# Block-sparse attention with a squared-ReLU feed-forward: putting off more squares and moving one slot's choices from a transfer to the matmul engine

## The chip, the cores and the metric

The kernel runs on one core of a Trainium2 chip. The metric is the device time of one execution in microseconds (us), the median of several runs. Five engines work side by side, each through its own queue in order: PE (TensorE: matmuls, and transposes as matmuls against an identity), DVE (VectorE), ACT (ScalarE), POOL (GpSimd) and SP (SyncE, which here only issues transfers). POOL issues the loads that convert f32 to bf16; SP issues the transposing transfers and the stores.

## The reference

For 4 batches and 8 heads, 768 rows and head size 64, each query row keeps the 6 best of 24 chunks of 32 keys. The bound of a chunk is computed from the minimum and maximum of its keys. Attention runs over the kept chunks, causally, and a feed-forward with squared ReLU follows.

```python
k_chunks = k.reshape(B, H, nc, chunk, D)
k_min = np.min(k_chunks, axis=3)
k_max = np.max(k_chunks, axis=3)
ub = np.sum(np.maximum(q[:, :, :, None, :] * k_min[:, :, None, :, :], q[:, :, :, None, :] * k_max[:, :, None, :, :]), axis=-1)
ub = np.where(causal, ub, -1000000000.0)
top_chunks = np.argsort(ub, axis=-1)[..., -top_k:]
scores = scale * np.matmul(q, k.transpose(0, 1, 3, 2))
sel = (j_chunk == top_chunks[..., None]).any(axis=-2)
mask = sel & (pos[:, None] >= pos[None, :])
# softmax over the masked scores, then attn @ v; then, row by row of x (3072 x 512):
h = np.maximum(x @ w_in, 0.0)
return (h * h @ w_out).astype(np.float32)
```

## The kernel before

The work is cut into 8 half-batches `hb` (384 query rows of one batch) in a fixed `ORDER`, and each into 4 slots, one for each pair of heads: 32 slots `s`, with `hb = s // 4`. A slot has these steps, and the main loop writes out by hand in which order the steps of neighbouring slots follow one another in each engine's queue:

- `step_T` transposes k and q on PE (half-batches 0 to 2). From half-batch 3 on (`ON_PE = 3`) SP does it by transposing transfers (`tr`, L320), six for each half-batch: three tiles of k and three of q.
- `extrema` or `step_K` (DVE) make the chunks' minima and maxima; `relus_T` or `relus` (L316, L317) make the positive and negative parts of q.
- `step_U` computes the bounds `ub` on PE (L371 to L382). The DVE then takes the sixth largest (MAX8, L389) and compares (L391): a 1 for each chunk that is not chosen.
- These choices have to stand transposed under the transposed q in the operand `kq`, as 32 further rows of the contraction, where a large negative weight pushes the chunks that were not chosen out of the softmax. `step_V` does that on PE for half-batches 0 to 2: it transposes into PSUM (L424 or L434) and the DVE copies (L428 or L439). From half-batch 3 on `step_Q` (L405) puts the q beside the choices in `nsel`, and `step_W` (L413) sends both through a transposing transfer on SP.
- `step_E` computes the scores (L452, PE), the exponential (L458, ACT) and the causal diagonal (L462, POOL).
- `step_F` multiplies with v (L480, PE) and divides (L489, L490, DVE) into `x`. `x` is transposed by SP (L494), or in a few slots by PE in `x_T` (L518) with a DVE copy (L524).

The feed-forward of a finished half-batch is pushed into a `queue` of 16 "up" steps (`ffn_up`, one for each f: L566 on PE, the ReLU L576 on ACT, the square L577 on the DVE) and 12 "down" steps (`ffn_down`, L589). The calls `f1()` take one step of it at a time and so place it between the attention's steps; `quota` says how many a slot takes. For the last four f of half-batch 0 the ReLU goes straight into `h` (L572) and the square is put into a list `squares`, which is worked off (L573) in slot 8.

Loads are listed by slot in `later` and issued by `go(s, n)`, at most n of them at each call. SP's transposing transfers stand in `first` (issued at the start of a slot) and `by_sp`. PSUM tiles of `psA` (tag `att`) have two buffers, shared by `ub`, `po` and `qt`.

Of the kernel before, what the change touches and what calls it, by code (L numbers as in the profile page):

```python
# [9 lines left out]
BF16 = mybir.dt.bfloat16  # L10
# [6 lines left out]
HT = 3  # L17
HB = HT * 128
# [12 lines left out]
ON_PE = 3  # L31
# [8 lines left out]
def kernel(  # L40
# [9 lines left out]
    nc = tc.nc  # L50
    B, H, S, D = q.shape
    NC = S // CH
    NT = S // 128
    NP = H // 2
# [3 lines left out]
    NFI = DFF // 128  # L58
# [12 lines left out]
    CR = CH  # L71
# [172 lines left out]
    def step_cast(n, p):  # L244
        if n == "k":
            nc.vector.tensor_copy(packed("k", 0)[:, 2 * p:2 * p + 2], staged["k", p])
        else:
            nc.scalar.copy(qn0[:, :, p, :, 0:D], staged["q", p])
# [161 lines left out]
    def step_W(s):  # L410

        b, half, p = slots[s]
        nc.sync.dma_start_transpose(  # L413
            out=kqs[b % 2][:, p, 2 * half + 1].rearrange("r h (j t) -> r (h j) t", j=HT),
            in_=nsel[half][:, s % 2].rearrange("r h j n d -> r (h j n d)"))

    def step_V(s):
        b, half, p = slots[s]
        if s < NP:

            qt = psA.tile([128, 2, HB], BF16, tag="att", name="qt")
            for hh in range(2):
                for j in range(HT):
                    nc.tensor.matmul(  # L424
                        qt[0:KR, hh, 128 * j:128 * (j + 1)],
                        lhsT=qn0[:, j, p, hh, :],
                        rhs=ident, is_transpose=True, start=True, stop=True)
            nc.vector.tensor_copy(kqs[b % 2][0:KR, p, 2 * half + 1], qt[0:KR])  # L428
            return
        j0 = 1 - half  # L430
        c = 128 * j0
        qt = psA.tile([128, HB], BF16, tag="att", name="qt")
        for j in range(j0, HT):
            nc.tensor.matmul(  # L434
                qt[0:2 * CR, 128 * j:128 * (j + 1)],
                lhsT=chosen[s % 2][:, j].rearrange("r h c -> r (h c)"),
                rhs=ident, is_transpose=True, start=True, stop=True)
        for h in range(2):
            nc.vector.tensor_copy(  # L439
                kqs[b % 2][D:KR, p, 2 * half + 1, h, c:], qt[CR * h:CR * h + CR, c:])  # L440

    def step_E(s, hh, n):
        b, half, p = slots[s]
# [119 lines left out]
    def ffn_up(hb, xT, f):  # L563
        ph = psF.tile([128, 512], F32, tag="ph", name="ph")
        for ki in range(NKI):
            nc.tensor.matmul(  # L566
                ph[:, 0:HB], lhsT=w_in[:, ki, 128 * f:128 * (f + 1)],
                rhs=xT[:, ki, :], start=(ki == 0), stop=(ki == NKI - 1))
        h = late.tile([128, HB], BF16, tag="h", bufs=2 * NFI + 2, name="h")
        if hb == 0 and f >= NFI - 4:  # L570
            h2[hb, f] = h
            nc.scalar.activation(h, ph[:, 0:HB], ACT.Relu)  # L572
            squares.append(lambda: nc.vector.tensor_mul(h, h, h))  # L573
            return
        ht = late.tile([128, HB], BF16, tag="ht", bufs=4, name="ht")
        nc.scalar.activation(ht, ph[:, 0:HB], ACT.Relu)  # L576
        nc.vector.tensor_mul(h, ht, ht)  # L577
        h2[hb, f] = h

    def ffn_down(hb, py, t, c, act, tail):  # L580
        if c == 0:
            if hb == 0 and t == 1:
                py[t] = psF.tile([128, DM], F32, tag="ph", name="py")
            elif tail:
                py[t] = psS.tile([128, DM], F32, tag="ps", name="py")
            else:
                py[t] = psY.tile([128, DM], F32, tag="py", name="py")
        for f in range(4 * c, 4 * c + 4):
            nc.tensor.matmul(  # L589
                py[t], lhsT=h2[hb, f][:, 128 * t:128 * (t + 1)], rhs=w_out[:, f, :],  # L590
                start=(f == 0), stop=(f == NFI - 1))
        if c == 3:
            ob = late.tile([128, DM], F32, tag="ob", bufs=3, name="ob")
            if act:
                nc.scalar.copy(ob, py[t])  # L595
            else:
                nc.vector.tensor_copy(ob, py[t])
            r0 = S * ORDER[hb][0] + HB * ORDER[hb][1] + 128 * t
            nc.sync.dma_start(out[r0:r0 + 128, :], ob)

    def fill(n, act):
        for _ in range(n):
# [6 lines left out]
    def at(s, fn, *a):  # L609
        later.setdefault(s, []).append(lambda: fn(*a))  # L610
# [22 lines left out]
    for j in range(HT):  # L633
        at(6, load_vt, 0, HT + j)
        at(7 + j // 2, load_n, "k", 3, j)
        at(8, load_n, "q", 3, j)
        at(9, load_vt, 1, HT + j)
    at(9, codes, 1, 1, nc.gpsimd.dma_start)
    for b in range(2, B):
        for g in range(2):  # L640
# [4 lines left out]
            at(4 * g - (7 if g == 4 else 8) + i // HT, load_n, "kq"[i // HT], g, i % HT)  # L645
    s0 = 4 * ON_PE - 3
    for i in range(2 * HT):
        first.setdefault(s0 + i // HT, []).append((tr, ON_PE, "kq"[i // HT], i % HT))
    first.setdefault(s0 + 2, []).append((place_dma, ON_PE))
    for g in range(ON_PE + 1, 2 * B):  # L650
        for j in range(HT):
# [4 lines left out]
    def go(s, n):  # L656
        for _ in range(n):
            if later.get(s):
                later[s].pop(0)()

    def busy(n, pool=psA, tag="att"):

        idle = pool.tile([128, 128], F32, tag=tag, name="idle")
        for _ in range(n):
            nc.tensor.matmul(idle, lhsT=ident, rhs=ident, start=True, stop=True)  # L665

    busy(28)
    step_cast("k", 0)
    blank(0, 1)
    step_cast("q", 0)  # L670
# [21 lines left out]
    extrema(1)  # L692
    step_T(2, F, Y, "k")
    extrema(2, 0)
    for i in range(2):
        nc.vector.memset(chosen[i], 0.0)
    early.close()
    late = ctx.enter_context(tc.tile_pool(name="late", bufs=2))
    for s in range(NP):
# [43 lines left out]
    for s, (b, half, p) in enumerate(slots):  # L743
# [16 lines left out]
        if s == NP:  # L760
# [8 lines left out]
            place(s + 1, "k", nc.vector.tensor_copy)  # L769
            place(s + 1, "q", nc.scalar.copy)  # L770
        if s == 2 * NP:
            for n in range(hf):
                step_E(s, 0, n)
            relus_T(s + 1)
            place(s + 1, "q", nc.scalar.copy)
            step_F(s - 1, 0)
            step_F(s - 1, 1)
            f1()
            x_T(1, 1, F, (1,))
            f1()  # L780
            extrema(s + 1)
            place(s + 1, "k", nc.vector.tensor_copy)
            for fn in squares:
                fn()
            x_copy(1, 1, 1, 2, nc.vector.tensor_copy)
            push(1)
        if p == 0 and hb > 2:
            step_F(s - 1, 0)
            step_F(s - 1, 1)
            push(hb - 1)  # L790
        else:
            f1()
# [8 lines left out]
        if hb > 1 and s != 2 * NP:  # L801
            f1()
        if hb < ON_PE:
            go(s, 2)
        for n in range(hf, nb):
            step_E(s, 0, n)
        if hb < ON_PE and p:
            k1()
        if s < NS - 2 or s + 1 == 3 * NP:
            step_U(s + (1 if hb < ON_PE else 2))  # L810
        if s + 1 == ON_PE * NP:
            step_W(s + 1)
        if hb >= ON_PE and s < NS - 2:
            step_W(s + 2)
        if ON_PE * NP - 4 <= s <= ON_PE * NP - 3:

            nc.vector.memset(
                nsel[1 - s % 2][:, :, :, :, 1, :]
                .rearrange("p i h j c -> p (i h j) c"), 0.0)
        late_f = half == 0 and hb > 2  # L820
        border = p == 0 and hb > 1
        if not border and not (late_f and p == NP - 1) and s + 1 != 2 * NP:
# [17 lines left out]
                f1()  # L840
        if not (late_f and p == 0):
            f1()
        if s + 1 < ON_PE * NP:
            step_V(s + 1)
        if hb == ON_PE and p == 0:
            parts.extend(step_K(hb + 1))
# [67 lines left out]
```

## Time and profile before

| | |
|---|---|
| time, median of 3 runs (lowest to highest) | 268.7 us (267.63 to 269.91) |
| the profiled execution | 268.67 us, its span 266.9 us |
| granted TensorE clock | 1.00 throughout |
| PE busy | 254.6 us (95%) |
| DVE / ACT / POOL busy | 163.4 / 177.3 / 93.4 us |

The span runs from the first to the last instruction of the profiled execution; what lies around it is 1.8 us. In the views below, a group of a timeline reads: start in us, duration in us, engine, line, operation, output<-inputs, shapes, count; in brackets the idle time of the engine before it and what ended that. In the groups by line, "| busy us, mean ns | idle us" follows the count.

In the timeline slot 4 begins at about 24 us, slot 8 near 47, slot 9 near 55, slot 10 near 64, slot 11 near 72 and slot 12 near 83.

### The profile page before, as it was taken

The numbers are of one execution on the slowest core, as the hardware profiler recorded it, in microseconds if no ns is written. First come the engines' busy times: TensorE is split into PE (matmuls) and PEld (weight loads), VectorE is DVE, ScalarE is ACT, GpSimd is POOL, SyncE is SP. The second block draws the span as 40 slices with busy tenths as digits, with TensorE's granted clock in tenths as the row PEclk, the third lists the DMA queues.
The fourth block names the chain that finished last, engine by engine and source line by source line (L and its number), as shares of the span: only waits on it lengthen the run. The fifth ranks groups of instructions, "written<-read, shape, count | busy, mean of one in ns | idle before, by whom it ended". The sixth has DMA issues, their size and how long they took to land.

```text
span 266.9 us, 6575 instructions
## 1 busy us (share of the span) xinstructions
PE 254.6 (95%) x2409; PEld 156.3 (59%) x2409; DVE 163.4 (61%) x618; ACT 177.3 (66%) x398; POOL 93.4 (35%) x140
## 2 busy tenths in 40 slices
PE   7878999999987999999999999999999999999995
PEld 6566565556654566655665566655565666645543
DVE  6889998858984458656875576555863233424411
ACT  5988887698864678845575787934685788614500
POOL 8997455447811425225621544320120111000000
PEclk9999999999999999999999999999999999999999
DMA  7999999999999699999996999995542220111022
GB/s 134 171 185 186 207 215 175 128 177 110 138 157 136 136 161 151 133 178 127 181 151 138 133 146 175 137 154 142 125 96 68 71 44 17 55 42 41 2 77 81
DMA packets 116433, 33.88 MB, mean 127 GB/s; under 512 B 103344, under 2 KB 112336, under 8 KB 116400
## 3 DMA queue, kind: packets, MB, share of 16 engines
q0 software_dynamic: 64672, 13.83, 65.9%
q1 hardware_dynamic: 50784, 19.23, 39.6%
q10 hardware_dynamic: 944, 0.39, 0.6%
q8 instruction: 19, 0.31, 0.5%
q14 instruction: 14, 0.11, 0.2%
HBM read 27.26 MB, written 6.29 MB: 126 GB/s over the span
## 4 chain that ended last, share of the span: by engine, by line
PE 79%; DVE 10%; DMA 5%; ACT 2%; issue 2%; SPq 1%; POOL 0%; DVEq 0%; POOLq 0%; ACTq 0%
PE py L589 29%; PE ph L566 24%; PE ps L452 11%; PE po L480 7%; DMA kqT<-qn 3%; DMA kq<-nsel 2%; PE idle L665 2%; PE ub L375 1%; PE py L554 1%; DVE h L577 1%; DVE kq L293 1%; PE tk L267 1%; SPq L320 1%; DVE km L336 1%; DVE x L490 1%
## 5 line engine op out<-in xcount | busy, mean ns | idle before, releaser
L458 ACT ACTIVATE e<-ps 128x512 bf16<-128x512 f32 x192 | 96.5, 551 | 21.3 <-PE ps L452 20.6
L566 PE MATMUL ph<-xT,w_in 128*128 128x384 bf16 x512 | 98.9, 325 | 0.3 <-ACT ht L576 0.2
L589 PE MATMUL py<-w_out,h 128*128 128x512 bf16 x368 | 88.1, 379 | 0.5 <-DVE kq L293 0.3
L577 DVE TENSOR_TENSOR h<-ht 128x384 bf16<-128x384 bf16 x124 | 45.5, 378 | 56.2 <-ACT ht L576 55.7
L462 POOL TENSOR_SCALAR_AFFINE_SELECT e<-e 128x384 bf16<-128x384 bf16 x64 | 34.0, 535 | 131.2 <-ACT e L458 131.1
L576 ACT ACTIVATE ht<-ph 128x384 bf16<-128x384 f32 x124 | 60.3, 501 | 28.6 <-PE ph L566 28.1
L566 PEld LDWEIGHTS <-w_in 128*128 128x128 bf16 x512 | 47.8, 97 | 30.9 <-issue 1.4
L452 PE MATMUL ps<-kq 96*128 96x384 bf16 (+2 forms) x320 | 57.6, 278 | 3.8 <-DVE kq L428 2.1
L589 PEld LDWEIGHTS <-h 128*128 128x128 bf16 x368 | 34.6, 97 | 35.6 <-issue 0.6
L452 PEld LDWEIGHTS <-kq 96*128 96x128 bf16 x320 | 26.3, 97 | 18.9 <-issue 4.1
L480 PEld LDWEIGHTS <-e 128*128 128x128 bf16 x672 | 25.3, 98 | 4.6 <-POOL e L462 0.5
L480 PE MATMUL po<-vn,e 128*128 128x65 bf16 x672 | 26.6, 193 | 0.4 <-DVE x L490 0.4
L389 DVE MAX8 m<-ub 128x8 f32<-128x16 f32 (+4 forms) x160 | 16.1, 165 | 15.8 <-PE ub L382 10.1
L595 ACT COPY ob<-py 128x512 f32<-128x512 f32 x18 | 10.5, 585 | 22.6 <-PE py L589 22.3
L490 DVE TENSOR_TENSOR x<-po,r 128x384 bf16<-128x384 f32 x32 | 17.8, 557 | 1.1
L109 POOL DMA_DIRECT2D kn<-in_k_dram x15 | 13.3, 895 | 0.6 <-issue 0.3
L109 POOL DMA_DIRECT2D qn<-in_q_dram x15 | 13.3, 892 | 0.2
L336 DVE TENSOR_TENSOR km<-km 128x384 bf16<-128x384 bf16 (+3 forms) x40 | 12.2, 306 | 1.1
L125 POOL DMA_DIRECT2D vn<-in_v_dram x15 | 12.5, 842 | 0.4 <-issue 0.4
L375 PE MATMUL ub<-kbd,qr 128*128 128x48 bf16 (+1 forms) x160 | 9.6, 180 | 1.9 <-DVE qr L316 1.2
L375 PEld LDWEIGHTS <-qr 128*128 128x128 bf16 x160 | 7.9, 96 | 5.8 <-DVE qr L316 2.4
L288 ACT ACTIVATE qr<-tq 128x256 bf16<-128x256 bf16 (+1 forms) x24 | 8.8, 422 | 0.7 <-PE tq L260 0.5
(73 smaller groups left out, 181.5 us busy)
## 6 DMA issues: line engine op xcount, KB each, us to landing
out_dram<-ob SPq DMA_DIRECT2D x23, 256.0 KB, 2.6
w_in<-in_moe_w_in_dram POOLq DMA_DIRECT2D x2, 1024.0 KB, 11.7
w_out<-in_moe_w_out_dram POOLq DMA_DIRECT2D x2, 1024.0 KB, 18.0
kn<-in_k_dram POOLq DMA_DIRECT2D x15, 128.0 KB, 5.7
qn<-in_q_dram POOLq DMA_DIRECT2D x15, 128.0 KB, 6.1
kq<-kqT SPq DMA_DIRECT2D x10, 192.0 KB, 5.1
vn<-in_v_dram POOLq DMA_DIRECT2D x4, 384.0 KB, 8.1
vn<-in_v_dram POOLq DMA_DIRECT2D x9, 128.0 KB, 9.1
```

Source lines behind the costliest of these rows:

```text
L109: nc.gpsimd.dma_start(out=nat_of(n, g)[:, DM * j:DM * j + DM].rearrange("p (h d) -> p h d", d=D), in_=rows(n, *ORDER[g], 0, H)[:, 128 * j: ...
L375: nc.tensor.matmul(ub[:, j - j0], lhsT=st[s]["qr"][:, w, 128 * j:128 * (j + 1)], rhs=kbds[b % 2][:, p, w, :, 0:ncs], start=bool(half) and ...
L389: nc.vector.max(out=m8[:, j, hh, :], in_=ub[:, j - j0, hh, 0:12 * half + 4 * j + 4])
L452: nc.tensor.matmul(ps[:, at:at + 128 * m], lhsT=kqs[b % 2][0:KR, p, 2 * (j // HT), hh, 128 * (j % HT):128 * (j % HT + 1)], rhs=qc(s, hh)[: ...
L458: nc.scalar.activation(e[:, 512 * n + lo:512 * n + hi], ps[:, lo:hi], ACT.Exp, scale=float(scale))
L462: nc.gpsimd.affine_select(out=d, in_=d, compare_op=ALU.is_ge, fill=0.0, base=0, channel_multiplier=-1, pattern=[[0, 3], [1, 128]])
L480: nc.tensor.matmul(po[:, hh, i, :], lhsT=t["e"][hh][:, c:c + 128], rhs=vn[b % 2][:, 2 * p + hh, j, :], start=(j == 0), stop=(j == iq))
L490: nc.vector.tensor_mul(x[:, p].rearrange("p j (h d) -> p h j d", h=2), po[:, :, :, 0:D], r.to_broadcast([128, 2, HT, D]))
L566: nc.tensor.matmul(ph[:, 0:HB], lhsT=w_in[:, ki, 128 * f:128 * (f + 1)], rhs=xT[:, ki, :], start=(ki == 0), stop=(ki == NKI - 1))
L576: nc.scalar.activation(ht, ph[:, 0:HB], ACT.Relu)
L577: nc.vector.tensor_mul(h, ht, ht)
L589: nc.tensor.matmul(py[t], lhsT=h2[hb, f][:, 128 * t:128 * (t + 1)], rhs=w_out[:, f, :], start=(f == 0), stop=(f == NFI - 1))
```

## The change

- More squares are put off: the last eight f of half-batch 0 (four before) and the last six of half-batch 1 (none before). `put_off(6)` works off the first six at the start of slot 8, the two others follow further down in slot 8; the six of half-batch 1 come in slot 12 behind `step_F(11)`.
- `step_V` transposes the choices of the two heads side by side, each into the same 32 partitions, with two transposes where one stood for both heads, and copies them with one instruction for two.
- Slot 12's choices and q go through `step_V` (six transposes on PE and one DVE copy) for `step_W`.
- All six transposing transfers of half-batch 3 are issued at the start of slot 9; the three of q stood at the start of slot 10.
- The four loads listed for slot 8 are issued at its first `go` (two and two before), the k load first.
- The two memsets of `chosen` move to the front; the two of the unused part of `nsel` both go to slot 8 (8 and 9 before).

```diff
     def step_V(s):
         b, half, p = slots[s]
-        if s < NP:
+        if s < NP or s == ON_PE * NP:
             qt = psA.tile([128, 2, HB], BF16, tag="att", name="qt")
             for hh in range(2):
                 for j in range(HT):
                     nc.tensor.matmul(
                         qt[0:KR, hh, 128 * j:128 * (j + 1)],
-                        lhsT=qn0[:, j, p, hh, :],
+                        lhsT=qn0[:, j, p, hh, :] if s < NP else
+                        nsel[half][:, s % 2, hh, j].rearrange("r n d -> r (n d)")[:, 0:KR],
                         rhs=ident, is_transpose=True, start=True, stop=True)
             nc.vector.tensor_copy(kqs[b % 2][0:KR, p, 2 * half + 1], qt[0:KR])
             return
         j0 = 1 - half
         c = 128 * j0
-        qt = psA.tile([128, HB], BF16, tag="att", name="qt")
-        for j in range(j0, HT):
-            nc.tensor.matmul(
-                qt[0:2 * CR, 128 * j:128 * (j + 1)],
-                lhsT=chosen[s % 2][:, j].rearrange("r h c -> r (h c)"),
-                rhs=ident, is_transpose=True, start=True, stop=True)
+        qt = psA.tile([128, 2, HB], BF16, tag="att", name="qt")
         for h in range(2):
-            nc.vector.tensor_copy(
-                kqs[b % 2][D:KR, p, 2 * half + 1, h, c:], qt[CR * h:CR * h + CR, c:])
+            for j in range(j0, HT):
+                nc.tensor.matmul(
+                    qt[0:CR, h, 128 * j:128 * (j + 1)], lhsT=chosen[s % 2][:, j, h],
+                    rhs=ident, is_transpose=True, start=True, stop=True)
+        nc.vector.tensor_copy(kqs[b % 2][D:KR, p, 2 * half + 1, :, c:], qt[0:CR, :, c:])
...
-        if hb == 0 and f >= NFI - 4:
+        if hb < 2 and f >= NFI - (8, 6)[hb]:
             h2[hb, f] = h
             nc.scalar.activation(h, ph[:, 0:HB], ACT.Relu)
             squares.append(lambda: nc.vector.tensor_mul(h, h, h))
...
+    def put_off(n=NFI):
+        for fn in squares[:n]:
+            fn()
+        del squares[:n]
...
     for j in range(HT):
         at(6, load_vt, 0, HT + j)
         at(7 + j // 2, load_n, "k", 3, j)
+        at(9, load_vt, 1, HT + j)
+    for j in range(HT):
         at(8, load_n, "q", 3, j)
-        at(9, load_vt, 1, HT + j)
...
     for i in range(2 * HT):
-        first.setdefault(s0 + i // HT, []).append((tr, ON_PE, "kq"[i // HT], i % HT))
+        first.setdefault(s0, []).append((tr, ON_PE, "kq"[i // HT], i % HT))
...
     busy(28)
+    for x in chosen:
+        nc.vector.memset(x, 0.0)
     step_cast("k", 0)
...
     extrema(2, 0)
-    for i in range(2):
-        nc.vector.memset(chosen[i], 0.0)
...
         if s == 2 * NP:
+            put_off(6)
             for n in range(hf):
                 step_E(s, 0, n)
...
-            for fn in squares:
-                fn()
+            put_off()
             x_copy(1, 1, 1, 2, nc.vector.tensor_copy)
             push(1)
         if p == 0 and hb > 2:
             step_F(s - 1, 0)
             step_F(s - 1, 1)
+            put_off()
             push(hb - 1)
...
-            go(s, 2)
+            go(s, 4 if s == 2 * NP else 2)
...
-        if s + 1 == ON_PE * NP:
-            step_W(s + 1)
         if hb >= ON_PE and s < NS - 2:
             step_W(s + 2)
-        if ON_PE * NP - 4 <= s <= ON_PE * NP - 3:
-            nc.vector.memset(
-                nsel[1 - s % 2][:, :, :, :, 1, :]
-                .rearrange("p i h j c -> p (i h j) c"), 0.0)
+        if s == 2 * NP:
+            for x in nsel:
+                nc.vector.memset(
+                    x[:, :, :, :, 1, :].rearrange("p i h j c -> p (i h j) c"), 0.0)
...
-        if s + 1 < ON_PE * NP:
+        if s + 1 <= ON_PE * NP:
             step_V(s + 1)
```

## The prediction

> **What bounds the kernel now.** I read the page first, then busy time by stretches, the waits, the chain that ended last, and the timelines of single engines.
>
> ```profile
> span 266.9 us, 6575 instructions
> PE 254.6 (95%) x2409; PEld 156.3 (59%) x2409; DVE 163.4 (61%) x618; ACT 177.3 (66%) x398; POOL 93.4 (35%) x140
> ```
>
> TensorE (PE) is busy 95% of the span. Two kinds of gain are left: the 12 us in which it is empty, and work on it that could go. The stretches (us; busy time of PE, PEld, DVE, ACT, POOL; granted clock) say where the empty time is.
>
> ```profile
> 0.00:23.00 23.00, 18.33 (x266) 14.24 (x267) 17.91 (x74) 18.03 (x47) 21.41 (x37) 1.00 1.28 167
> 23.00:43.00 20.00, 19.18 (x226) 12.21 (x223) 19.01 (x62) 17.40 (x43) 11.07 (x17) 1.00 1.36 204
> 75.00:90.00 15.00, 12.23 (x138) 7.87 (x138) 8.79 (x46) 7.89 (x18) 1.15 (x3) 1.00 1.28 144
> 90.00:230.00 140.00, 139.60 (x1270) 85.56 (x1268) 80.76 (x325) 97.97 (x214) 42.12 (x61) 1.00 1.01 126
> ```
>
> From 90 us on PE is full: what is won or lost before 90 us stays to the end, and nothing in the diff works after it. From 23 to 43 us VectorE (DVE) is busy 19.01 of 20 us, so there it decides with PE. From 75 to 90 us PE lacks nearly 3 us. The chain shows what that is.
>
> ```profile
> 66.91 8.89 DMA kqT<-qn
> 75.92 0.12 DVE qr L316
> 78.33 5.38 DMA kq<-nsel
> 83.86 0.60 PE ps L452 x4
> ```
>
> Two transfers in a row end late. The transposed q of half-batch 3 lands at 75.80, and the DVE's `relus(12)` (L316) starts on it. The transposed choices of slot 12 (L413) land at 83.71, and the scores of slot 12 wait for them. The edit attacks both: the q transposes are issued a slot earlier, and slot 12's choices go through PE and the DVE instead.
>
> **Part by part.** The sum is made against the profiled execution: 268.67 us, of which 266.9 are its span; it lies at the median of the runs shown (268.7).
>
> *The price of one more transpose and of one copy.* These rows are PE and DVE groups of the timeline, and the copies by shape:
>
> ```profile
> 22.01 0.30 PE L434 MATMUL qt<-ident,chosen 128*64 128x128 bf16 x2
> 45.59 0.35 PE L434 MATMUL qt<-ident,chosen 128*64 128x128 bf16 x3
> 14.44 0.51 PE L424 MATMUL qt<-ident,qn 128*96 128x128 bf16 x6
> L439 DVE COPY kq<-qt 32x384 bf16<-32x384 bf16 x8 | 2.8, 351 | 2.1 <-PE qt L434 1.9
> L439 DVE COPY kq<-qt 32x256 bf16<-32x256 bf16 x8 | 2.3, 284 | 0.3
> L428 DVE COPY kq<-qt 96x768 bf16<-96x768 bf16 x4 | 2.2, 551 | 0.8 <-PE qt L424 0.8
> ```
>
> A third transpose adds 0.05 us, and so does each from three to six ((0.51 - 0.35) / 3). The new ones are 32 wide, a width the trace lacks; from below they could cost half (0.027), from above their weight load alone (0.109, the row further down). I take 0.053, as both widths shown agree. Per slot there are 2 more (slots 4 to 7) or 3 more (8 to 11): 0.11 or 0.16 us. Two copies become one: by the slope of the two rows (67 ns per 128 elements) 32x768 costs 351 + 3 x 67 = 552 ns, which is what L428 takes. A pair of 384s takes 0.73 us (row at 45.99 below), so the DVE saves 0.18 us per slot; the output's strides I price at nothing, with 0.1 either way.
>
> *The memsets.* The two of `chosen` end just when the MAX8 behind them could start anyway, since that waits for PE's `ub`; at the front they find the DVE idle for 0.45 us before the first cast.
>
> ```profile
> L434 PEld LDWEIGHTS <-chosen 128*64 128x64 bf16 x20 | 1.3, 108 | 2.9 <-DVE chosen L391 1.0 <-issue 0.7 <-DVE r L489 0.6
> 3.84 0.42 DVE L246 CAST kn<-stage 96x512 bf16<-96x512 f32 x1 [0.45 <-DMA stage<-in_k_dram]
> L696 DVE MEMSET chosen<- 128x96 uint32 x2 | 0.2, 138 | 0.0
> 54.52 0.73 DVE L439 COPY kq<-qt 32x384 bf16<-32x384 bf16 x2 [1.10 <-PE qt L434]
> ```
>
> So nothing there; without either cover it would be 0.2 us. The second `nsel` memset now also falls into slot 8, where the DVE waits 1.10 us for PE: nothing again.
>
> *Slots 5 to 7 (29 to 44 us).* The newly put-off squares f8 to f11 were these DVE rows; the PE rows show what PE then waited for:
>
> ```profile
> 34.89 0.35 DVE L577 TENSOR_TENSOR h<-ht 128x384 bf16<-128x384 bf16 x1
> 38.59 0.61 DVE L577 TENSOR_TENSOR h<-ht 128x384 bf16<-128x384 bf16 x2
> 37.34 0.19 PE L371 MATMUL ub<-cmask,ident 128*128 128x48 bf16 x1
> 37.69 0.25 PE L375 MATMUL ub<-kbd,qr 128*128 128x24 bf16 x4 [0.16 <-DVE kbd L233]
> 42.69 0.53 PE L480 MATMUL po<-vn,e 128*128 128x65 bf16 x12
> 43.54 1.04 PE L589 MATMUL py<-w_out,h 128*128 128x512 bf16 x4 [0.32 <-DVE kq L293]
> ```
>
> With four squares (1.3 us) and three copies' 0.18 us gone the DVE runs 0.6 to 1.4 us ahead, and both waits end. An emptied PE also loses the filling of its pipeline, so I count from start to start: 37.34 to 37.69 less 0.03 for one short matmul, and 42.69 to 43.54 less 0.38 for twelve L480 matmuls (thirty take 0.96, below): 0.32 and 0.47. That is -0.8; six more transposes give back 0.3 (slot 4's two fall where PE waits anyway): **-0.5**.
>
> *Slot 8, where the squares go.* `put_off(6)` stands in the DVE's queue between the copy of `step_V(8)` and the reciprocal of `step_F(7)`; queued behind it are x(7), extrema(9), the placing of k(9). PE itself waits for x(7) in `x_T` (L518).
>
> ```profile
> 45.99 0.73 DVE L439 COPY kq<-qt 32x384 bf16<-32x384 bf16 x2 [0.82 <-PE qt L434]
> 47.69 0.20 DVE L489 RECIPROCAL r<-po 128x6 f32<-128x6 f32 x1 [0.97 <-PE po L480]
> 48.53 0.34 PE L518 MATMUL pt<-ident,x 128*128 128x128 bf16 x3
> 50.58 1.15 DVE L573 TENSOR_TENSOR h<-h 128x384 bf16<-128x384 bf16 x4
> L577 DVE TENSOR_TENSOR h<-ht x124: 295/358/860, 27.2 to 253.8; 128x384 bf16<-128x384 bf16 x124
> 46.71 0.52 POOL L462 TENSOR_SCALAR_AFFINE_SELECT e<-e 128x384 bf16<-128x384 bf16 x1 [1.72 <-ACT e L458]
> ```
>
> Four squares take 1.15 us, a further one 0.27, so six take 1.6. The slowest square of the trace took 860 ns instead of about 350; a POOL select of 0.52 us falls among the six, so I add 0.5. Idle time covers 0.97 and the shorter copy 0.18; about 0.95 of 2.1 us is left. PE would reach `x_T` that much too early: I take +0.8, between 0.2 (no hold) and the rival's price below. Three more transposes: +0.16. Squares f14 and f15 follow later, and the next choices have a margin of the 1.10 us seen above. **+0.95**.
>
> The Trainium skill (SBUF — State Buffer, Who interferes with whom) says that a DVE instruction with two SBUF inputs contends with a GpSimd instruction that reads SBUF, and not with one that only writes it; whoever is first keeps the shared ports to its end. By that rule the four loads that POOL now issues in one go hold no square, and the six can meet this select and at most one more, which caps them at 1.6 + 2 x 0.52 = 2.6 us. No run here shows yet which it is; I lower the slow rival's chance for it.
>
> *Slots 9 and 10.* Three more transposes each, PE being full there: **+0.32**.
>
> *Slot 11's start: the q transposes.* SP issues three k transposes in slot 9 and three q ones in slot 10; now six in slot 9.
>
> ```profile
> 55.29 6.24 SPq L320 DMA_TRANSPOSE kqT<-kn x3
> 64.23 4.90 SPq L320 DMA_TRANSPOSE kqT<-qn x3
> DMA to landing us min/median/max: 2.4/4.8/8.9
> 75.92 0.26 DVE L316 TENSOR_SCALAR qr<-kqT 128x384 bf16<-128x384 bf16 x1 [0.44 <-DMA kqT<-qn]
> 76.24 0.47 PE L375 MATMUL ub<-kbd,qr 128*128 128x48 bf16 x6 [1.17 <-DVE qr L316]
> ```
>
> The first three took 6.24 us because the third k load came late; all four loads of slot 8 are now issued in its first `go`. Six transposes at 1.2 to 2.2 us end near 64 us, 8.9 more is 73: before the DVE gets there. Behind them on SP stands one x transpose of slot 8 (62.96), needed only after 90 us. But the DVE is no more than 0.44 us from its own bound here: it works without a gap from 63.66 to 75.49. It saves two copies' 0.36 as well, so `relus(12)` starts 0.8 earlier, and PE, which lost 1.3 us here, wins **-0.8**, slot 11's own transposes included.
>
> *Slot 12's choices.* The 5.38 us of the transfer go off the path. In its place stand six transposes 96 wide on PE (0.32, with the switch of tile shape some 0.44) and one DVE copy of 0.55. PE comes to them at about 78.5, after the DVE's comparison (L391, 78.00 before, earlier now); the copy ends 2 us before it is needed.
>
> ```profile
> 81.13 1.12 PE L480 MATMUL po<-vn,e 128*128 128x65 bf16 x30
> 83.86 0.60 PE L452 MATMUL ps<-kq 96*128 96x384 bf16 x4 [1.60 <-DMA kq<-nsel]
> 88.49 0.61 DVE L389 MAX8 m<-ub 128x8 f32<-128x16 f32 x6 [3.53 <-PE ub L382]
> ```
>
> Thirty such matmuls take 0.96 us (their busy time less the last one's drain), so 83.86 could be 82.09: -1.77 + 0.44 = **-1.33**. SP is also rid of one 1.4 us issue. The six squares of half-batch 1 (1.6 us) fall into the 3.53 us in which the DVE waits. The third of the four down steps behind them needs f10 some 1.7 us after the first begins; margin about 1 us, so nothing, and up to 0.8 without it.
>
> The sum: -0.5 + 0.95 + 0.32 - 0.8 - 1.33 = -1.36, or **267.3 us**.
>
> **The rivals.** (a) The moved work is all hidden: the six squares fit (0.95 becomes 0.16 or less) and slots 9 and 10 absorb their transposes in PE's small gaps: -0.5 - 0.8 - 1.33 = -2.6, **266.1**. For it: the DVE idles 0.82 and 0.97 us in slot 8. Against it: the six stand behind the first of these gaps. (b) A wait is replaced by a like one: the q transposes land no earlier (the longest took 8.9 us), or slot 12's scores wait for the DVE's copy; the -0.8 goes and half of the -1.33: **268.8**, no change. Then the change wouldn't do what it says. (c) Slower: the six squares of slot 8 are held as long as the slowest square, 6 x 0.86 = 5.2 us instead of 2.1; x(7) and `x_T` come 3.1 us later than in my sum: **270.4**. It decides once the six take over 2.1 + 1.36 = 3.5 us. For it: the squares run next to POOL's selects and loads. Against it: the median square is 358 ns and POOL's stretch there holds two selects.
>
> **How the numbers follow.** Forecast 0.48, (a) 0.26, (b) 0.12, (c) 0.14. Unknown costs: 15 uncovered transposes at 0.027 to 0.109 give -0.4 to +0.8; slot 8 gives -0.8 to +0.5 short of (c); the runs spread by about 1 either way. Range 265.1 to 269.7, reaching to (a) and (b) and part of (c). About 1% (2.7 us) is what can be told from no change: faster by more asks for (a) with a little luck, or a forecast whose unknown costs fall low, 0.27; slower by more is (c) and what I don't see, 0.16; within it 0.57.
>
> **What would show it.** Right: no PE wait for `kq<-nsel` near 82 us and none for L316 above 0.5 us near 75; an L518 wait near 48 us that grew to about 1 us; the squares of slot 8 at 0.27 to 0.35 us but for one or two; 32-wide transposes 0.053 apart; PE as full after 90 us as now. Wrong: PE's last score of slot 12 not about 1.5 us earlier than before, or the gain lost again after 90 us.

## The result, and the profile after

The changed kernel takes 267.42 us (median of 13 runs, 266.94 to 267.66) against 268.59 us for the kernel before (13 runs taken beside them, 267.63 to 271.13). The ratio is 0.9946 with a 95% interval of 0.9926 to 0.9967: about 1.2 us or half a per cent faster, and inside the 1% that the prediction called no change. The profiled execution took 267.35 us, 265.6 of them its span, against 268.67 and 266.9 before.

First the page of the changed kernel: the span, and each engine's busy time.

```profile
span 265.6 us, 6581 instructions
PE 254.1 (96%) x2409; PEld 157.4 (59%) x2435; DVE 163.4 (62%) x611; ACT 177.7 (67%) x398; POOL 94.0 (35%) x140
```

The same stretches as before (us; busy time of PE, PEld, DVE, ACT, POOL; granted clock):

```profile
23.00:43.00 20.00, 19.09 (x221) 12.07 (x218) 17.18 (x54) 17.13 (x42) 11.17 (x18) 1.00 1.36 204
75.00:90.00 15.00, 14.66 (x158) 9.32 (x157) 11.29 (x53) 9.90 (x21) 1.99 (x4) 1.00 0.85 137
90.00:230.00 140.00, 138.59 (x1253) 85.61 (x1269) 80.58 (x322) 98.43 (x215) 42.22 (x61) 1.00 1.05 125
```

DVE has lost 1.8 us of work between 23 and 43 us, and PE is no busier for it (19.09 against 19.18). From 75 to 90 us PE went from 12.23 to 14.66 us: there lies the gain. From 90 us on it is as full as before: the same matmul stands 0.81 us ahead at 83.9 us and 0.80 us ahead at 226 (table below). Its busy time is lower there because the trace lacks some matmul records (1253 against 1270 in this stretch).

The places of the prediction in PE's timeline:

```profile
38.22 0.81 PE L566 MATMUL ph<-xT,w_in 128*128 128x384 bf16 x4 [0.25 <-ACT h L572]
...
43.06 0.53 PE L480 MATMUL po<-vn,e 128*128 128x65 bf16 x12
43.51 1.04 PE L589 MATMUL py<-w_out,h 128*128 128x512 bf16 x3
...
45.56 0.51 PE L437 MATMUL qt<-ident,chosen 128*32 128x128 bf16 x6
...
49.47 0.34 PE L518 MATMUL pt<-ident,x 128*128 128x128 bf16 x3 [0.76 <-DVE x L490]
...
76.86 0.47 PE L375 MATMUL ub<-kbd,qr 128*128 128x48 bf16 x6 [0.29 <-DVE qr L316]
...
79.89 0.50 PE L424 MATMUL qt<-ident,nsel 128*96 128x128 bf16 x6
...
82.09 1.12 PE L480 MATMUL po<-vn,e 128*128 128x65 bf16 x30
83.05 0.60 PE L452 MATMUL ps<-kq 96*128 96x384 bf16 x4
```

The wait of 0.32 us ahead of L589 (43.5) is gone. The one ahead of L375 (37.69 before) is gone too, but a new one of 0.25 us stands right behind it, for ACT's ReLU (L572). `x_T` (L518), which waited for nothing, now waits 0.76 us for `x`. The wait for `qr` fell from 1.17 to 0.29 us, and the 1.60 us for `kq<-nsel` have gone: the scores (83.05) follow the weighted sums (82.09) without a wait.

On DVE, in the same stretches:

```profile
46.11 0.55 DVE L440 COPY kq<-qt 32x768 bf16<-32x768 bf16 x1 [0.97 <-PE qt L437]
46.69 2.02 DVE L573 TENSOR_TENSOR h<-h 128x384 bf16<-128x384 bf16 x6
48.64 0.18 DVE L489 RECIPROCAL r<-po 128x6 f32<-128x6 f32 x1
...
76.56 0.25 DVE L316 TENSOR_SCALAR qr<-kqT 128x384 bf16<-128x384 bf16 x1
...
80.43 0.55 DVE L429 COPY kq<-qt 96x768 bf16<-96x768 bf16 x1
...
83.95 2.01 DVE L573 TENSOR_TENSOR h<-h 128x384 bf16<-128x384 bf16 x6
87.69 0.61 DVE L389 MAX8 m<-ub 128x8 f32<-128x16 f32 x6 [1.72 <-PE ub L382]
```

The six squares of slot 8 take 2.02 us, and the reciprocal behind them no longer finds a gap. The six of slot 12 fit into DVE's idle time, of which 1.72 us are left.

To see where time is won and lost, the start of the same matmul is compared in two traces. The table gives "this kernel minus the kernel before", in us, at places named by their time before; a number that falls along a row is a gain. (The kernels other than "after" are the experiments below.)

| kernel | 24.6 front | 41.5 slot 7 | 44.4 just before `step_V(8)` | 48.5 `x_T` | 63.2 slot 10 | 72.8 slot 11 | 76.2 `ub` of slot 12 | 79.3 | 83.9 scores of slot 12 | 226 |
|---|---|---|---|---|---|---|---|---|---|---|
| after | +0.35 | +0.38 | -0.03 | +0.93 | +1.24 | +1.50 | +0.62 | +0.96 | -0.81 | -0.80 |
| before, again | +0.57 | +0.38 | +0.38 | +0.38 | +0.38 | +0.81 | +0.17 | +0.17 | -0.40 | -0.40 |
| after, again | +0.27 | +0.34 | -0.07 | +0.89 | +1.20 | +1.47 | +0.59 | +0.92 | -0.85 | -0.85 |
| x_first | +0.47 | +0.52 | +0.11 | +0.27 | +1.08 | +1.34 | +0.46 | +0.79 | -0.97 | -0.97 |
| squares_as_before | +1.85 | +1.88 | +1.57 | +1.72 | +2.03 | +2.29 | +1.41 | +1.74 | -0.02 | -0.02 |
| q_transposes_late | +0.65 | +0.69 | +0.28 | +1.24 | +1.55 | +1.81 | +0.93 | +1.27 | -0.50 | -0.50 |
| slot12_by_transfer | +0.76 | +1.12 | +0.71 | +1.67 | +1.98 | +2.24 | +1.36 | +1.36 | -0.21 | -0.21 |
| choices_as_before | +0.27 | 0.00 | -0.33 | +1.13 | +1.13 | +1.19 | +0.60 | +0.93 | -0.84 | -0.83 |
| moves_only | +0.59 | +0.39 | +0.39 | +0.39 | +0.39 | +0.45 | -0.14 | +0.19 | -1.57 | -1.56 |
| moves_only_again | +0.28 | +0.44 | +0.45 | +0.45 | +0.45 | +0.51 | -0.09 | +0.25 | -1.52 | -0.89 |
| squares_in_gaps | +1.00 | +1.11 | +0.77 | +0.83 | +0.83 | +0.89 | +0.30 | +0.63 | -1.14 | -1.13 |
| slot12_alone | +1.05 | +0.97 | +0.98 | +0.98 | +0.97 | +1.13 | +0.65 | +0.98 | -0.78 | -0.78 |
| one_more_transfer | +0.26 | +0.28 | -0.13 | +0.83 | +1.14 | +1.40 | +0.52 | +0.86 | -0.91 | -0.91 |

The front column differs between executions of one kernel (the kernel before by 0.57), so a row is read from there; the trace of the kernel before, to which all are compared, has the earliest front of the fourteen. The last number and the span also differ: PE of the changed kernel is 0.80 us ahead at the end, but its span is 1.2 us shorter. The rest comes behind the last matmul: 3.49 us from its start to the end of the span before, 3.07 us after.

### The profile page after: what moved, and what is told of

Same layout as the page of the kernel before. It is cut to its first block, busy times and chain, and to the rows that moved or that the text cites. A ratio compares the mean times of both kernels' runs of the same rounds, so it can differ in the third digit from the quotient of the medians.

```text
span 265.6 us, 6581 instructions
## 1 busy us (share of the span) xinstructions
PE 254.1 (96%) x2409; PEld 157.4 (59%) x2435; DVE 163.4 (62%) x611; ACT 177.7 (67%) x398; POOL 94.0 (35%) x140
## 4 chain that ended last, share of the span: by engine, by line
PE 81%; DVE 10%; ACT 5%; issue 3%; POOL 1%; DVEq 0%; ACTq 0%; POOLq 0%
PE py L589 28%; PE ph L566 26%; PE ps L452 11%; PE po L480 7%; PE idle L671 2%; DVE km L336 2%; ACT e L458 2%; PE ub L375 2%; PE py L554 1%; DVE h L577 1%; ACT ht L576 1%; DVE x L490 1%; PE tk L267 1%; DVE kq L429 1%; DVE h L573 1%
## 5 line engine op out<-in xcount | busy, mean ns | idle before, releaser
L589 PE MATMUL py<-w_out,h 128*128 128x512 bf16 x342 | 82.9, 379 | 1.9 <-issue 0.3
L577 DVE TENSOR_TENSOR h<-ht 128x384 bf16<-128x384 bf16 x114 | 42.1, 378 | 55.4 <-ACT ht L576 54.9
L576 ACT ACTIVATE ht<-ph 128x384 bf16<-128x384 f32 x114 | 55.5, 500 | 26.7 <-PE ph L566 26.2
L589 PEld LDWEIGHTS <-h 128*128 128x128 bf16 x368 | 34.7, 97 | 35.2 <-issue 0.6
L375 PE MATMUL ub<-kbd,qr 128*128 128x48 bf16 (+1 forms) x160 | 9.8, 180 | 0.7 <-DVE qr L316 0.3
L375 PEld LDWEIGHTS <-qr 128*128 128x128 bf16 x160 | 7.7, 96 | 4.3 <-DVE qr L316 1.5
```

What stands on the lines that cost most here:

```text
L375: nc.tensor.matmul(ub[:, j - j0], lhsT=st[s]["qr"][:, w, 128 * j:128 * (j + 1)], rhs=kbds[b % 2][:, p, w, :, 0:ncs], start=bool(half) and ...
L589: nc.tensor.matmul(py[t], lhsT=h2[hb, f][:, 128 * t:128 * (t + 1)], rhs=w_out[:, f, :], start=(f == 0), stop=(f == NFI - 1))
```

## The experiments

**The kernel before, profiled again**, with the changed kernel again in the same set (267.46 us, 267.19 to 268.41; ratio 0.9963, 0.9942 to 0.9984). No edit.

> The kernel before, for its profile alone. In the two profiles at hand PE stands 0.25 to 0.35 us later in the changed kernel from 23 us on, where a POOL select ends later, and the time from the last matmul to the end of the span is 0.5 us shorter. Theory: both are differences from run to run and not of the change, so this profile shows the first matmul of po behind 22.9 us anywhere within 0.4 us of the two, and the tail behind the last store anywhere from 2.1 to 2.7 us. Rival: both belong to the change, and this profile repeats the numbers of before within 0.05 us (23.29 us for the fourth reciprocal, 2.6 us of tail).

> The changed kernel, as the base for the kernels beside it. Theory (the sum over slots): about 1.2 us less than before, 267.4. Rival (the gain is only what PE's shift shows behind 90 us, 0.8 us): 267.8.

The kernel before gave 268.22 us in the one execution measured, 3.50 us behind the last matmul, and a front that differs by 0.57: the front is chance from run to run, the tail, which was expected to be chance too, is not. This second trace has another lesson in its waits (its timelines of DVE, SP and PE):

```profile
76.11 0.25 DVE L316 TENSOR_SCALAR qr<-kqT 128x384 bf16<-128x384 bf16 x1
```

```profile
78.51 1.25 SPq L413 DMA_TRANSPOSE kq<-nsel  x1
```

```profile
83.46 0.60 PE L452 MATMUL ps<-kq 96*128 96x384 bf16 x4 [1.03 <-DMA kq<-nsel]
```

The transfer was issued 0.18 us later than before (78.33) and its result was there 0.4 us earlier (PE goes on at 83.46 instead of 83.86), and DVE found q landed. A kernel that comes later to such a landing waits less: the two landings absorb what was lost earlier. With no edit at all this row goes from +0.57 at the front to -0.40 at the end, so the gain of a changed kernel depends by some tenths of a us on which execution of the kernel before it is held against.

**x first** moves the six squares of slot 8 behind the division that makes x.

```
-            put_off(6)
             for n in range(hf):
                 step_E(s, 0, n)
...
             step_F(s - 1, 1)
+            put_off(6)
```

> The changed kernel with the first six squares of slot 8 behind the reciprocal and x of slot 7 in the DVE's queue instead of ahead of them. Theory (these squares delay x(7), and PE waits 0.76 us for it in the transposes of x): the wait goes, the shift of PE at the transposes of x falls from +0.93 to about +0.2, and the time is 0.6 to 0.8 us less than the changed kernel's: 266.7. Rival (the wait only moves, to the down steps that need f8 to f11, to the squares' successors on the DVE or to the next choices): a new wait of 0.5 us or more between 49 and 56 us and the same time as the changed kernel, 267.4.

267.71 us (266.93 to 269.68), ratio 0.9968 (0.9944 to 0.9992): not less than after. In PE's timeline the wait for x has gone and another has come:

```profile
48.80 0.34 PE L518 MATMUL pt<-ident,x 128*128 128x128 bf16 x3
...
52.64 0.38 PE L452 MATMUL ps<-kq 96*128 96x384 bf16 x2 [0.31 <-ACT e L458]
```

In the table, it loses 0.16 us from 44.4 us to `x_T` instead of 0.96, but then 0.81 to slot 10 instead of 0.31: 0.97 against 1.27 in all. Most of what the squares cost only moved, to a wait for ACT's exponentials; the 0.3 us left over does not show in the time.

**Squares as before** keeps everything but the squares: four are put off instead of eight and six.

```
-        if hb < 2 and f >= NFI - (8, 6)[hb]:
+        if hb == 0 and f >= NFI - 4:
...
-            put_off(6)
```

> The changed kernel with only the four squares put off that were put off before, at their old place; all other parts of the change stay. Theory (putting off more squares wins 0.3 to 0.5 us in slots 5 to 7 and loses 0.7 to 0.8 in slot 8): 0.3 to 0.5 us less than the changed kernel, 267.0, with PE waits for the DVE back near 37.7 and 43.5 us and none at the transposes of x near 48.5. Rival (the relief of the DVE up to 45 us is what the change lives on): 0.5 us or more over the changed kernel, 267.9 or more.

266.75 us (266.53 to 268.14), ratio 0.9943 (0.9922 to 0.9963), where after took 267.46 in the same set. PE's timeline of it:

```profile
45.11 1.04 PE L589 MATMUL py<-w_out,h 128*128 128x512 bf16 x3
...
50.26 0.34 PE L518 MATMUL pt<-ident,x 128*128 128x128 bf16 x3
```

Neither wait is there, although the first was expected back. Slot 8 costs no more than its three transposes (+1.57 to +1.72), and the wait ahead of L589, at 43.5 before, ended without any further square put off (+1.88 to +1.57): in this trace the single copies do that alone. The profiled execution began 1.85 us late (its granted clock was 0.65 from 10 to 15 us and 0.67 from 15 to 20) and yet ended level, a gain of 1.87 us from front to end against 1.15 for after. So the squares put off lose about 0.7 us, on PE and in the time.

**The q transposes late**: all of the change, but three k transposes in slot 9 and three q transposes in slot 10, as before.

```
-        first.setdefault(s0, []).append((tr, ON_PE, "kq"[i // HT], i % HT))
+        first.setdefault(s0 + i // HT, []).append((tr, ON_PE, "kq"[i // HT], i % HT))
```

> The changed kernel with the three transposing transfers of q of half-batch 3 back at the start of slot 10; the loads stay early. Theory (the DVE reaches its work on this q only 0.3 to 0.5 us before the transfer landed in the profile of before, since its own queue is its next bound): 0.3 to 0.6 us over the changed kernel, 267.9, with the DVE's wait for kqT back near 76 us. Rival (the transfer was the whole bound): the full PE wait of 1.2 us is back and the time is 0.9 us or more over the changed kernel, 268.3 or more. Second rival (the early loads alone suffice, or slot 12 has slack for it): no difference.

267.59 us (266.8 to 270.36), ratio 0.9943 (0.9911 to 0.9976). Its DVE timeline where q is used:

```profile
76.33 0.62 DVE L342 TENSOR_TENSOR kbd<-km,hmask 128x48 bf16<-128x48 bf16 x2
76.87 0.25 DVE L316 TENSOR_SCALAR qr<-kqT 128x384 bf16<-128x384 bf16 x1
```

The expectation failed, and its second rival holds: DVE comes to L316 out of its own queue, without a wait. The trace's semaphore records have the last q tile landing at 76.22 us here, 0.65 us ahead of DVE, and at 68.44 in after. From slot 11 to `ub` the kernel wins 0.88 us, as after does. In the changed kernel the early q transposes bring nothing.

**Slot 12 by transfer**: all of the change, but slot 12's choices go through `step_W`, as before.

```
-        if s < NP or s == ON_PE * NP:
+        if s < NP:
...
+        if s + 1 == ON_PE * NP:
+            step_W(s + 1)
...
-        if s + 1 <= ON_PE * NP:
+        if s + 1 < ON_PE * NP:
```

> The changed kernel with slot 12's choices and q through the transposing transfer on SP again. Theory (the transfer's 5.4 us end on the path, PE's replacement costs 0.35 us): PE waits 1.5 to 1.8 us for kq near 82 us and the time is 1.2 to 1.5 us over the changed kernel, 268.8. Rival (with the q transposes out of SP's way the transfer ends in time): the wait is below 0.5 us and the time at most that of the changed kernel.

267.9 us (267.13 to 270.19), ratio 0.9967 (0.9938 to 0.9995): 0.4 to 0.5 us above after, where more than 1 was expected. Its timelines of SP and PE:

```profile
79.11 1.24 SPq L413 DMA_TRANSPOSE kq<-nsel  x1
```

```profile
82.49 1.12 PE L480 MATMUL po<-vn,e 128*128 128x65 bf16 x30
83.65 0.60 PE L452 MATMUL ps<-kq 96*128 96x384 bf16 x4
```

The transfer began 0.78 us later than before and PE could go on at 83.65, 0.21 us earlier. In three traces it was issued at 78.33, 78.51 and 79.11, and the scores began at 83.86, 83.46 and 83.65: they hardly follow the issue. PE was 1.36 us late here, so nearly nothing of the wait was left, and the transfer costs little. Most of the 0.4 us can be the tail: 3.49 us behind the last matmul, as before.

**Choices as before**: all of the change, but with the 64-wide transpose and two copies in `step_V` for slots 4 to 11.

```
-                    qt[0:CR, h, 128 * j:128 * (j + 1)], lhsT=chosen[s % 2][:, j, h],
+                lhsT=chosen[s % 2][:, j].rearrange("r h c -> r (h c)"),
...
-        nc.vector.tensor_copy(kqs[b % 2][D:KR, p, 2 * half + 1, :, c:], qt[0:CR, :, c:])
+            nc.vector.tensor_copy(
+                kqs[b % 2][D:KR, p, 2 * half + 1, h, c:], qt[CR * h:CR * h + CR, c:])
```

> The changed kernel with the choices of slots 4 to 11 transposed and copied as before: half as many transposes, two copies for one. Theory (each of the new transposes costs PE 0.05 us: 0.15 us per slot from 8 on; the single copy saves the DVE 0.18 us, which counts only where PE waits for the DVE, in slots 5 to 7 and at the start of slot 11): PE wins 0.45 us in slots 8 to 10 and loses about 0.2 to 0.4 at the DVE's bounds, so within 0.3 us of the changed kernel, 267.3. Rival (the single copy is a gain that shows): 0.5 us or more over the changed kernel.

267.48 us (267.04 to 269.22), ratio 0.995 (0.9918 to 0.9981): the same as after, as expected. The table shows why. Slots 5 to 7 win 0.60 instead of 0.38, without the added transposes there; slot 8 costs 1.46 instead of 0.96; slots 9 and 10 cost nothing instead of 0.31; slot 11 wins less. From the front to the end it is -1.10 against -1.15.

**The moves alone**: squares and choices as before (the two edits above together); left are slot 12's choices on PE, the early loads and q transposes, and the memsets.

> The kernel before with the moves alone: slot 12's choices on PE, the q transposes and the loads earlier, the memsets at their new places; squares, and choices of slots 4 to 11, as before. Theory (the sum over slots: -0.45 at the start of slot 11, -1.43 in slot 12, and none of slot 8's cost): 1.8 us less than before, 266.8, and so 0.5 us less than the changed kernel. Rival (the DVE's backlog of slots 8 to 11 eats the earlier q): no faster than the changed kernel, 267.4.

> The moves alone once more, beside the two kernels built on them. Theory: 2.2 us less than before, 266.3, PE 1.9 us ahead of its own start offset from slot 12 on and a tail of 3.07 us. Rival (the first measurement was favoured by its chip): at most 1.5 us less than before.

266.29 us (265.93 to 266.94), ratio 0.9897 (0.9855 to 0.9938), and in another set 266.55 (265.98 to 268.25), ratio 0.9937 (0.9909 to 0.9965): 0.9 to 1.1 us below after, although the intervals of the ratios overlap. From 41.5 us to the scores of slot 12 PE gains 1.96 and 1.97 us in the two traces, all of it from slot 11 on; after gains 1.19. In the second one PE lost 0.62 us again near 123 us, at the start of a feed-forward that waited for a transposing transfer of x:

```profile
122.16 0.49 PE L568 MATMUL ph<-xT,w_in 128*128 128x384 bf16 x2
122.83 0.76 PE L568 MATMUL ph<-xT,w_in 128*128 128x384 bf16 x2 [0.19 <-DMA xT<-x]
```

So PE is not full after 90 us in every execution.

**Slot 12 alone**: the kernel before with nothing but slot 12's choices on PE.

```
-        if s < NP:
+        if s < NP or s == ON_PE * NP:
...
-                        lhsT=qn0[:, j, p, hh, :],
+                        lhsT=qn0[:, j, p, hh, :] if s < NP else
+                        nsel[half][:, s % 2, hh, j].rearrange("r n d -> r (n d)")[:, 0:KR],
...
-        if s + 1 == ON_PE * NP:
-            step_W(s + 1)
...
-        if s + 1 < ON_PE * NP:
+        if s + 1 <= ON_PE * NP:
```

> The kernel before with slot 12's choices and q on PE and nothing else of the change. Theory (5.4 us of transfer off the path: -1.77 + 0.34 on PE, and -0.43 in the tail): 1.5 to 1.9 us less than before, 266.9, and 0.3 to 0.5 more than the moves alone, which save the DVE's wait for the transposed q besides. Rival (the q transposes and loads add nothing, since the DVE reaches the q no sooner): the same time as the moves alone, 266.4. Second rival (what was gained from the transfer needs the earlier q): 1 us or less below before.

266.94 us (266.37 to 267.37), ratio 0.9939 (0.9916 to 0.9963). Its PE timeline:

```profile
76.89 0.47 PE L375 MATMUL ub<-kbd,qr 128*128 128x48 bf16 x6 [0.69 <-DVE qr L316]
...
82.11 1.12 PE L481 MATMUL po<-vn,e 128*128 128x65 bf16 x30
83.07 0.60 PE L453 MATMUL ps<-kq 96*128 96x384 bf16 x4
```

This one edit has the whole gain of the change: +0.33 for the transposes, -1.76 for the wait, and the shorter tail (3.06 us). Whether the early q transposes and loads add something to it is not settled: the moves alone took 266.55 us in the same set, but the runs of the two overlap. In this trace the last q tile lands at 76.45 us and L316 starts 0.12 us behind it, as in the kernel before; in the moves alone DVE starts L316 at 75.79 and 75.85.

**Squares in gaps**: the moves alone, and eight squares of half-batch 0 put off but worked off in three lots: two ahead of slot 8's choices, two at its start, four where the kernel before has its four.

```
-        if hb == 0 and f >= NFI - 4:
+        if hb == 0 and f >= NFI - 8:
...
+            put_off(2)
...
+        if s == 2 * NP - 1:
+            put_off(2)
         if s + 1 <= ON_PE * NP:
             step_V(s + 1)
```

> The kernel with the moves alone, and eight squares of half-batch 0 put off as in the change, but worked off where the DVE waits for PE: two before the copy of step_V(8) in slot 7, two after it, four at the old place further down in slot 8; none of half-batch 1. Theory (putting off f8 to f11 ends PE's wait near 43.5 us, about 0.4 us, and costs nothing where the squares have a cover): 0.3 to 0.4 us less than the moves alone, 265.9, and no L518 wait above 0.2 us. Rival (x(7) or the copy of step_V(8) is delayed all the same): as the moves alone or more, 266.3 or over, with the wait before L518 or before the scores of slot 8.

266.55 us (265.83 to 267.69), ratio 0.9932 (0.991 to 0.9955), the same as the moves alone in that set. PE's timeline:

```profile
44.31 1.04 PE L591 MATMUL py<-w_out,h 128*128 128x512 bf16 x3
...
49.36 0.34 PE L520 MATMUL pt<-ident,x 128*128 128x128 bf16 x3
```

The wait ahead of L591 (the kernel before's L589) has gone (-0.34), and `x_T` waits for nothing (+0.06): two squares fit where six don't. What that wins on PE does not show in the time, so the expected 0.3 to 0.4 us did not come.

**One more transfer**: the changed kernel with one of SP's transfers (L306, near slot 11) cut in two.

```
+            for p0, p1 in ((0, 2), (2, NP)) if g == ON_PE and h else ((0, NP),):
...
-                    out=kqs[b % 2][0:D, :, 2 * half, h, :],
+                    out=kqs[b % 2][0:D, p0:p1, 2 * half, h, :],
```

> The changed kernel with one more transfer on SP: the second of the two copies that place half-batch 3's k (slot 11) is split in two. In the profiles so far the time from the last matmul's start to the end of the span is 3.49 us where slot 12's choices go by transfer and 3.07 where they do not; SP ends with waits on a fixed list of semaphores, and the last store's lands second on the list in the first case and last in the second. Theory (the transfers of SP and ACT take these semaphores in turn, so one transfer fewer moves the last store to the end of the list, and the waits behind it are no longer left over): one transfer more brings 3.49 us back, with PE's own times unchanged; 0.4 us over the changed kernel, 267.9. Rival (the shorter tail belongs to the missing transposing transfer itself, or to chance): 3.07 us stays, 267.4.

267.81 us (267.42 to 268.48), ratio 0.9972 (0.9958 to 0.9985). PE moves as in after (-0.91 at the end), but the time behind the last matmul is 3.49 us again. The trace's semaphore records say why. SP ends with waits on semaphores, in pairs and in a fixed order; the transfers of SP and ACT take eight of these in turn. In us after the start of the last matmul:

```
                     before   after   one more transfer
last store lands on  sem 100  118     100
wait (100, 112)      2.16     1.02    as before
six more pairs to
(117, 101)           2.53     1.80    as before
wait (118, 115)      2.59     2.17    as before
span ends            3.49     3.07    3.49
```

The last store lands at about 2.15 us in both kernels. Where its semaphore is the second of the list, seven more waits of 0.06 us follow; where it is the last, none does. The change has one transfer fewer (slot 12's transpose), which turned the rotation by one.

## Why the prediction was right, and where it wasn't

The forecast was 267.3 us, the median 267.42, the profiled execution 267.35. The steps, as the prediction put them:

- **Prices of one transpose and one copy.** Right. The groups of the changed kernel by shape:

```profile
L437 PEld LDWEIGHTS <-chosen 128*32 128x32 bf16 x40 | 2.2, 96 | 2.6 <-DVE x L490 0.7 <-DVE chosen L391 0.5 <-DVE nsel L823 0.4
L440 DVE COPY kq<-qt 32x768 bf16<-32x768 bf16 x4 | 2.2, 548 | 1.9 <-PE qt L437 1.8
L440 DVE COPY kq<-qt 32x512 bf16<-32x512 bf16 x4 | 1.7, 416 | 0.7 <-PE qt L437 0.6
```

  The copy takes 548 ns where 552 was worked out; each of the slots 8 to 10 shows +0.15 to +0.16 us for its three more transposes, although the weight load alone takes 96 ns: it overlaps the matmuls before it.
- **Slots 5 to 7, -0.5.** Measured -0.38 from the front to 44.4 us. The step that was too large is the wait at 37.69: it turned into one for ACT's ReLU, 0.25 us, and PE stands at +0.38 at 41.5 us where the front had left it at +0.35; how much of it paid for the transposes can't be told from the front's scatter. The wait at 43.5 brought 0.41. Its cause was in part misnamed: the single copies were enough for it (squares_as_before), and so were the squares put off (choices_as_before); with neither, in the moves alone, it stands.
- **Slot 8, +0.95.** Measured +0.96. Squares 2.02 us against 2.1, L518's wait 0.76 against 0.8. Two small errors met in the 2.1: six squares without a hold come to 1.15 + 2 x 0.27 = 1.69 by the prediction's own rows, not 1.6, and the hold took 0.33 where 0.5 was added. Which select holds a square is seen in POOL's timeline and, below it, in narrow pieces of DVE's:

```profile
46.84 0.59 POOL L462 TENSOR_SCALAR_AFFINE_SELECT e<-e 128x384 bf16<-128x384 bf16 x1 [1.46 <-ACT e L458]
48.49 0.60 POOL L462 TENSOR_SCALAR_AFFINE_SELECT e<-e 128x384 bf16<-128x384 bf16 x1 [1.06 <-ACT e L458]
```

```profile
46.69 0.95 DVE L573 TENSOR_TENSOR h<-h 128x384 bf16<-128x384 bf16 x2
...
48.10 0.61 DVE L573 TENSOR_TENSOR h<-h 128x384 bf16<-128x384 bf16 x2
```

  By line, with the shortest, median and longest in ns:

```profile
L573 DVE TENSOR_TENSOR h<-h x14: 343/348/674, 46.7 to 85.6; 128x384 bf16<-128x384 bf16 x14
```

  The second square, which came while the select of 46.84 ran, took 0.67 us instead of 0.34; the pair at 48.10, of which the second ran when the next select came, took the usual 0.61. Both selects took 0.6 us instead of the 0.52 of the row before. The Trainium skill (SBUF — State Buffer, Who interferes with whom) has it that whoever is first keeps the shared ports to its end; this trace agrees, with one square held and not two, and with it rival (c), every square held, had no ground.
- **Slots 9 and 10, +0.32.** Measured +0.31.
- **Slot 11's start, -0.8.** Measured -0.62, its own transposes included. The size is near, the reason was wrong in part: I put the early q transposes first, and without them the gain is the same. It comes from DVE's own queue, which is shorter by two copies (with the two copies back, slot 11 to `ub` wins 0.59 instead of 0.88), and from DVE coming later than before to a landing that moved less than it did. The landings, where the q transposes stand in slot 10, are at 75.80, 75.59, 76.22 and 76.45 us in four traces; the wait of 0.44 us is listed in the first alone. The kernel before itself shows -0.21 over this stretch in its second trace, where DVE comes to L316 0.52 us behind the landing: the price of the q transposes rested on one execution.
- **Slot 12, -1.33.** Measured -1.43: -1.77 as worked out, and +0.34 for the transposes where 0.44 was priced. The -1.77 is again that one execution's: in the second trace of the kernel before the same wait is 1.03 us instead of 1.60. The six squares there cost nothing; DVE had 1.72 us left.
- **The memsets, 0.** Not separable: the front differs from run to run by more than they could cost.
- **Not in the sum:** the front, +0.35 in this execution, and the tail, -0.42. They nearly cancel, so the forecast of the total lay closer than its parts: these add to -1.15 on PE where -1.36 was said.

That the total came so close is luck. Of the 1.17 us between the medians the tail has 0.42 (if it is in every execution as in the two traces of each kernel), which the sum did not hold; that leaves 0.75 us for PE where 1.36 was forecast. The sum priced the two waits of slots 11 and 12 (1.17 and 1.60 us) at their size in one execution with the earliest front; in the second trace they are 0.53 and 1.03, and against it the changed kernel's PE is 0.40 us ahead at the end instead of 0.80. The prediction's own sign of being wrong points the same way: the scores of slot 12 were to come about 1.5 us earlier and came 0.81 earlier (83.05 against 83.86). The direction, the place of the gain and the cost of slot 8 were right.

Of the rivals, (a) failed where it put the six squares into the gaps; (b) on the q transposes, which land at 68.44 us instead of 75.80, and on slot 12's scores, which wait for nothing now. What (a) described, hidden work at 266.1 us, is about what the moves alone measured without the squares.

## What to carry to other kernels

Work put off has to be priced where it lands: six squares in a row at the head of a queue cost PE about 0.8 us through one engine's wait (0.96 with the three transposes there), more than the waits that they ended; two at a time cost 0.06. An edit that removes the last wait of a stage can be worth more alone than in company (here a transfer: 1.6 us alone, 0.4 to 0.5 when it is taken back out of the whole change), because while that wait stands it absorbs losses before it, and once it is gone these count. A wait for a landing is also an unsafe price: it is smaller in an execution that comes later to it, so look at it in more than one trace before it goes into a sum. So take the change apart and measure its parts even when the whole is faster.

## What the runs showed of the hardware

The time between the last store's landing and the end of the program depends on which semaphore the store happened to use: 0.42 us between second and last of the list, turned here by one transfer more or fewer in SP's queue. A difference of that size between two kernels need not come from their work. In SP's timeline of the kernel before, of after and of the one with one more transfer, the last store itself shows no difference but in its start:

```profile
263.95 0.33 SPq L560 DMA_DIRECT2D out_dram<-ob  x1
```

```profile
263.15 0.33 SPq L560 DMA_DIRECT2D out_dram<-ob  x1
```

```profile
263.04 0.33 SPq L561 DMA_DIRECT2D out_dram<-ob  x1
```

With spans of 266.87, 265.64 and 265.95 us, 2.91, 2.49 and 2.91 us follow its start. And a transposing transfer's landing followed its issue only in part: for slot 12's choices the issues lie 0.78 us apart in three traces and the scores start within 0.40 us; for the last q tile the issues lie 1.11 us apart in four traces (66.91 to 68.02) and the landings 0.86 (75.59 to 76.45). What sets it, no run here took apart.
